# The order of all operations as a searched list in place of a list scheduler; bonus sums on quarters of the array, a combine over four row groups, the first unit in four loads

## The chip, the cores and the metric

One NeuronCore of a Trainium2 chip runs the kernel. The metric is the device time of one execution in microseconds; shorter is better. Two executions that differ by less than some 2% can't be told apart here.

## The reference

A linear-attention layer (one decaying state per head) is followed by a soft mixture of experts. All tensors are f32: batch 4, 8 heads, 768 steps, head dimension 48, so the second part sees 3072 tokens of 384 features, with 8 experts of 4 slots and hidden size 1024.

```python
for t in range(S):                          # attention, per batch and head
    cur = einsum('bhd,bhe->bhde', u[None] * kt, vt)
    y[:, :, t] = einsum('bhd,bhde->bhe', rt, state + cur)
    state = wt[:, :, :, None] * state + einsum('bhd,bhe->bhde', kt, vt)
...
logits = x @ phi                            # mixture, over all 3072 tokens
d = softmax(logits, axis=0); slot_input = d.T @ x
slot_out[e] = maximum(slot_input[e] @ w1[e], 0) @ w2[e]
out = softmax(logits, axis=1) @ slot_out
```

## The kernel before

**The attention** is cut into 6 chunks of 128 steps and worked on in 16 pairs of heads, four per batch. Decays, keys and receptances come in 12 units (three per batch; each holds one pair and a third of the batch's fourth pair, which small transfers gather later). A unit is loaded as `wu` (387 KB) and `kru` (774 KB, keys and receptances side by side); VectorE makes running products of the decays (`F` and `E`, scans at L896 and L902, a reciprocal between them) and multiplies keys and receptances by them in place (`KR`, L908). Since `KR` overwrites its input, it waits for GpSimd's product of receptances and keys (`rk`, L893), from which TensorE makes the bonus sums (`bonus`, L917; ScalarE copies them out, L921).

Each pair then does on TensorE: `sc` (scores of a half, L1012, twice), `kn` (keys turned, L966), `U` (outer products of the chunks, L985), `AV` (scores by values, L1030, twice) and `in` (the part from the state, L1042). Between them ScalarE copies scores out (`at`, L1018), GpSimd masks them (`mask`, L1020) and scales values (`av`, L994), VectorE scans the states (`S`, L989) and adds up the pair (`y`, L1046). After four pairs the batch goes through the first part of the mixture: transposes (`xT`, L320), logits (`lg`, L336), a running maximum and exponentials, and slot sums (`smm`, L383); row softmaxes on the side (`rows`, `rsub`, `rmul`).

**The tail** spreads the slots (L450 to L482), multiplies by the first expert weights (`up`, L496), turns the result, multiplies by the second (`down`, L556, in three column groups of 160, 160 and 64), copies the rows to four places (`rep`, L566) and combines (`mix`, L582: six products of 32 rows by 128 columns per call, two row groups at a time, four calls per column group, in turn in two tiles of two banks, `cu` and `yp`). Evictions (L593, L595) and twelve output transfers follow.

**The order** is made on the host when the program is built. Each operation has an engine, a cost, a key (a due time) and the buffers it touches; `Plan.schedule` always takes the operation that can start first, with a slack within which the smaller key goes first, and the program is written out in that order. On the chip each engine, SyncE's transfer issues among them, works through its own list strictly in order, and waits on semaphores. `Plan.fill` puts products of zeros (L1211) into TensorE's longer planned gaps. PSUM has four single banks (`tp`), and the tiles `cu` and `yp`. The first unit is loaded and worked on in two halves of its columns; a half of `kru` is two separate strips of the tile (keys and receptances).

## Time and profile before

| what | value |
| --- | --- |
| median of 3 runs | 234.37 us (233.75 to 237.42) |
| profiled execution, its own time | 235.6 us |
| its span, first to last instruction | 233.9 us |
| TensorE / VectorE / GpSimd / ScalarE busy | 195.7 / 113.3 / 90.4 / 77.3 us |
| mean granted TensorE clock | 0.907 of 2.4 GHz |
| moved by DMA | 52.01 MB |

TensorE's busy time holds 21.7 us of products of zeros, and products that ran at half the clock. The engines' clocks and times below all come from the one profiled execution; a place is given in microseconds from the start of its span.

### The profile page before, as it was taken

To read this page: it belongs to the slowest core of one execution; us is meant where nothing else is said; L and a number is where in the kernel's file an instruction comes from. 1 tells how busy PE (TensorE), PEld (TensorE's weight loads), DVE (VectorE), ACT (ScalarE), POOL (GpSimd) and SP (SyncE) were. 2 spreads that over 40 slices of the span, in tenths; PEclk is the share of its full clock that TensorE was granted. 3 is DMA by queue.
4 is the path that set the end of the run, shared out by engine and by line. 5 is a ranking of instruction groups with operands and counts; after the bars stand their busy time and mean duration, and the time that the engine had idled before them with its cause. 6 is when DMAs were issued, how large, how long until landed. Compare 5 with 4: busy or idle time off the path is not lost.

```text
span 233.9 us, 9696 instructions
## 1 busy us (share of the span) xinstructions
PE 195.7 (84%) x4357; PEld 147.7 (63%) x4368; DVE 113.3 (48%) x162; ACT 77.3 (33%) x215; POOL 90.4 (39%) x126
## 2 busy tenths in 40 slices
PE   7379799888999787998978998979778889999870
PEld 2177667768757677865767884858665232588760
DVE  6196449775675375189547566352111310334340
ACT  0233215451525333343534655335312200313130
POOL 1256612842518575451757781384523000000000
PEclk9965979996899995899999999999958979999995
DMA  4799967998879699381656332129942935967193
GB/s 136 267 400 340 331 251 235 347 343 250 226 241 369 156 365 358 131 224 53 188 100 219 99 87 38 53 36 314 356 197 29 372 141 159 418 236 280 63 354 134
DMA packets 16049, 52.01 MB, mean 222 GB/s; under 512 B 2304, under 2 KB 3584, under 8 KB 16000
## 3 DMA queue, kind: packets, MB, share of 16 engines
q1 hardware_dynamic: 16000, 51.31, 65.1%
q8 instruction: 36, 0.59, 1.0%
q14 instruction: 13, 0.11, 0.2%
HBM read 44.21 MB, written 4.72 MB: 209 GB/s over the span
## 4 chain that ended last, share of the span: by engine, by line
PE 68%; POOL 9%; issue 7%; DMA 5%; DVE 4%; ACT 4%; SPq 0%; DVEq 0%; POOLq 0%
PE bank L1012 13%; PE bank L1030 11%; PE bank L1042 7%; POOL arena L1020 5%; PE bank L496 5%; PE bank L556 5%; PE bank L320 4%; PE bank L985 4%; PE bank L966 4%; DMA arena<-in_kru_dram 4%; PE bank L582 3%; PE bank L917 3%; PE bank L1211 3%; PE bank L336 2%; PE bank L383 2%
## 5 line engine op out<-in xcount | busy, mean ns | idle before, releaser
L1020 POOL TENSOR_SCALAR_AFFINE_SELECT arena<-arena 128x384 f32<-128x384 f32 x64 | 42.2, 683 | 61.6 <-ACT arena L1018 61.6
L1018 ACT COPY arena<-bank 128x384 f32<-128x384 f32 x64 | 27.5, 483 | 49.6 <-PE bank L1012 49.6
L1012 PE MATMUL bank<-arena 48*64 48x128 f32 x768 | 36.5, 306 | 7.2 <-issue 6.9
L1030 PE MATMUL bank<-arena 128*64 128x48 f32 x768 | 33.2, 236 | 7.3 <-POOL arena L1020 5.0
L1030 PEld LDWEIGHTS bank<-arena 128*64 128x64 f32 x768 | 28.7, 149 | 13.8 <-POOL arena L1020 7.9
L1012 PEld LDWEIGHTS bank<-arena 48*64 48x64 f32 x768 | 27.2, 151 | 13.8 <-issue 10.0
L908 DVE TENSOR_TENSOR arena<-arena 128x1548 f32<-128x1548 f32 (+1 forms) x13 | 24.6, 1893 | 7.8 <-POOL arena L893 7.2
L1046 DVE TENSOR_TENSOR arena<-bank,arena 128x576 f32<-128x576 f32 x16 | 12.0, 753 | 32.0 <-PE bank L1042 32.0
L893 POOL TENSOR_TENSOR arena<-arena 128x774 f32<-128x774 f32 (+1 forms) x13 | 18.9, 1453 | 21.8 <-PE bank L917 12.8
L989 DVE TENSOR_TENSOR_SCAN arena<-bank,arena 112x288 f32<-112x288 f32 x16 | 12.0, 749 | 26.1 <-PE bank L985 24.2
L1211 PE MATMUL bank<-zb 128*128 128x512 bf16 x69 | 21.7, 433 | 2.7 <-DVE bank L823 1.3
L896 DVE TENSOR_TENSOR_SCAN arena<-arena,bank 128x774 f32<-128x774 f32 (+1 forms) x13 | 21.2, 1633 | 1.3 <-DMA arena<-in_wu_dram 1.3
L902 DVE TENSOR_TENSOR_SCAN arena<-arena,bank 128x774 f32<-128x774 f32 (+1 forms) x13 | 21.3, 1640 | 0.4
L994 POOL TENSOR_TENSOR arena<-arena 128x576 f32<-128x576 f32 x16 | 18.5, 1156 | 1.5 <-ACT arena L921 1.4
L1042 PE MATMUL bank<-arena 48*64 48x48 f32 x640 | 17.9, 267 | 0.7 <-issue 0.7
L1042 PEld LDWEIGHTS bank<-arena 48*64 48x64 f32 x640 | 14.6, 150 | 1.9 <-issue 1.1
L917 PE MATMUL bank<-ub,arena 128*64 128x4 f32 x288 | 11.4, 208 | 5.0 <-DMA ub<-in_ub_dram 5.0
L966 PE MATMUL bank<-ident,arena 48*64 48x48 f32 x640 | 14.4, 234 | 0.9 <-issue 0.9
L917 PEld LDWEIGHTS bank<-ub,arena 128*64 128x64 f32 x288 | 10.6, 152 | 6.6 <-POOL arena L893 5.5
L966 PEld LDWEIGHTS bank<-ident,arena 48*64 48x64 f32 x640 | 13.8, 151 | 1.3 <-issue 1.0
L324 ACT COPY arena<-bank 128x384 f32<-128x384 f32 x24 | 10.6, 491 | 11.9 <-PE bank L320 11.9
L1211 PEld LDWEIGHTS <-zb 128*128 128x128 bf16 x80 | 7.7, 107 | 10.7 <-issue 4.8
(107 smaller groups left out, 211.3 us busy)
## 6 DMA issues: line engine op xcount, KB each, us to landing
arena<-in_w_dram SPq DMA_DIRECT2D x24, 512.0 KB, 7.7
arena<-in_w_dram SPq DMA_DIRECT2D x16, 640.0 KB, 6.6
arena<-in_kru_dram SPq DMA_DIRECT2D x11, 774.0 KB, 6.5
arena<-in_vp_dram SPq DMA_DIRECT2D x16, 288.0 KB, 3.3
arena<-in_wu_dram SPq DMA_DIRECT2D x11, 387.0 KB, 5.1
out_dram<-arena SPq DMA_DIRECT2D x8, 480.0 KB, 4.2
arena<-arena SPq DMA_DIRECT2D x24, 96.8 KB, 3.4
arena<-in_w_dram SPq DMA_DIRECT2D x8, 256.0 KB, 7.6
```

Source lines behind the costliest of these rows:

```text
L893: pl.op("POOL", 1.83 * wd / UW, lambda lo=lo, hi=hi: nc.gpsimd.tensor_tensor(out=rk.t[:, lo:hi], in0=r_of()[:, lo:hi], in1=k_of()[:, lo:hi ...
L896: pl.op("DVE", 0.07 + 1.7 * wd / UW, lambda lo=lo, hi=hi: nc.vector.tensor_tensor_scan(out=F_OF(q)[:, 1 + lo:1 + hi], data0=E_OF(q)[:, lo: ...
L902: pl.op("DVE", 0.07 + 1.7 * wd / UW, lambda lo=lo, hi=hi: nc.vector.tensor_tensor_scan(out=E_OF(q)[:, lo:hi][:, ::-1], data0=E_OF(q)[:, lo ...
L908: nc.vector.tensor_tensor(out=both(kr.t, lo, hi), in0=both(kr.t, lo, hi), in1=fac, op=ALU.mult)
L917: nc.tensor.matmul(out=ap.t[64 * th:64 * th + 64, c * 4:c * 4 + 4], lhsT=chunk(rk.t, c)[:, 64 * th:64 * th + 64], rhs=ub[:, j, :], start=T ...
L966: nc.tensor.matmul(out=kps[h].t[cols, c * D:(c + 1) * D], lhsT=chunk(K_OF(head(h)), c)[:, cols], rhs=ident[head(h), head(h)], start=True, ...
L1012: nc.tensor.matmul(out=aps[h].t[cols, cc * P:(cc + 1) * P], lhsT=chunk(K_OF(head(h)), 3 * hf + cc)[:, cols], rhs=chunk(R_OF(head(h)), 3 * ...
L1018: pl.op("ACT", 0.49, lambda h=h, aps=aps, ats=ats: nc.scalar.copy(out=ats[h].t, in_=aps[h].t[:, 0:3 * P]), r=[aps[h]], w=[ats[h]], key=kk, ...
L1020: pl.op("POOL", 0.55, lambda h=h, ats=ats: nc.gpsimd.affine_select(out=ats[h].t.rearrange("p (c t) -> p c t", c=3), in_=ats[h].t.rearrange ...
L1030: nc.tensor.matmul(out=yp.t[cols, 512 * h + c * D:512 * h + (c + 1) * D], lhsT=ats[h].t[:, cc * P + 64 * th:cc * P + 64 * th + 64], rhs=v4 ...
L1042: nc.tensor.matmul(out=yp.t[cols, 512 * h + c * D:512 * h + (c + 1) * D], lhsT=chunk(R_OF(head(h)), c)[:, cols], rhs=se[head(h), :, c], st ...
L1211: nc.tensor.matmul(out=tile[:, 0:512], lhsT=zb[:, 0:P], rhs=zb, start=True, stop=True)
```

## The change

1. `Plan.schedule` and all keys, due times and slacks go. `ORDER`, a constant list of the 788 operations by number, is written into the kernel, and `arrange` only replays it: it gives out the buffers and works out the planned times, which `fill` needs for the products of zeros. Costs of many operations are restated (for example `in` 0.58 to 0.80, `mask` 0.55 to 0.60), transfers are planned at most eight deep, and `near` adds a dependence, in the planned times alone, between `y` and `xT` of one batch.
2. `bonus`: 12 products of all 128 rows become 24 of 64 rows, in four quarters of the array, into two banks rather than one, with two copies by ScalarE.
3. `mix`: the four calls per column group become two, each of 12 products over four row groups; the first goes to `cu` and `yp`, the second to all four `tp` banks.
4. The first unit's `kru` comes in four pieces, each one strip of the tile, and `KR` of that unit is done for keys and receptances apart. Decoded, the list begins SyncE's queue with `wu` of unit 0 in two halves, `wu` of unit 1, `ub`, `kru` of unit 1, values of pair 1, and then the four pieces; TensorE's begins with `bonus1`, `sc1.0`, `sc0.0`. On GpSimd the row softmax of the first batch (`rsub0`) comes after the masks of pair 11 and those of batches 1 and 2 after the last pair; on TensorE `lg2`, `dturn2`, `smm2` and `rows1` stand between the steps of batch 3 (`AV15.1`, `xT3.0.1`, `lg2`, two more `xT3`, `in15`, `xT3.0.0`, `dturn2`, two more `xT3`, `lg3`, `smm2`, `rows1`, `dturn3`, `spread`, `rows3`, `smm3`, `den`, `slots`, `up00`); in the tail the order is `down00`, `down01`, `down10`, `rep0`, `down11`, `mix0.0`, `cturn1`, `rep1`, `mix1.1`, `mix1.0`, `down20`, `down21`, `fsum`, `mix0.1`, `rep2`, `mix2.0`, `mix2.1`.

```diff
-    def schedule(self):
+    def arrange(self, order):
...
+        for n in order:
+            o = self.ops[n]
+            assert all(p in done for p in o.preds), o.name
+            t = free[o.eng]
             for h in o.allocs:
...
+            for p in near.get(o, ()):
+                if p in done:
+                    t = max(t, reach(p, o.eng))
...
+            if o.eng == "SP":
+                if len(sent) >= self.DEEP:
+                    t = max(t, sent[-self.DEEP].end)
+                sent.append(o)
...
+            if n == 0:
+                for m in range(2):
+                    pl.op("SP", 0.42, dma(lambda lo=lo, hi=hi, m=m: q["kr"].t[:, m * UW + lo:m * UW + hi],
+                                          kru[n][:, m * UW + lo:m * UW + hi]), w=[(q["kr"], (i, m))],
+                          name=f"ld_kr{n}.{i}{m}", kb=(hi - lo) * 0.65)
+                continue
...
-                    nc.tensor.matmul(out=ap.t[64 * th:64 * th + 64, c * 4:c * 4 + 4], lhsT=chunk(rk.t, c)[:, 64 * th:64 * th + 64],
-                                     rhs=ub[:, j, :], start=True, stop=True)
+                    for h in range(2):
+                        cols, rows = slice(64 * th, 64 * th + 64), slice(64 * h, 64 * h + 64)
+                        nc.tensor.matmul(out=aps[h].t[cols, 2 * c:2 * c + 2], lhsT=chunk(rk.t, c)[rows, cols],
+                                         rhs=ub[rows, j, 2 * h:2 * h + 2], start=True, stop=True)
...
+                mx = [pl.new("tp") for _ in range(4)] if i else [pl.new("cu"), pl.new("yp")]
...
+                def mix(i=i, mv=mv, lo=lo, wd=wd):
+                    for j in range(3):
+                        for q in range(4):
+                            rows_ = slice(32 * q, 32 * q + NS)
+                            nc.tensor.matmul(out=mv(q)[:, j * wd:(j + 1) * wd], lhsT=cT[rows_, (3 * i + j) * P:(3 * i + j + 1) * P],
+                                             rhs=parts[rows_, lo:lo + wd], start=(j == 0), stop=(j == 2))
```

## Rows read from the trace of the kernel before

**Rows 1.** Busy time by stretch: length, engines (instructions), clock, DMA share, GB/s

```profile
14.80:27.30 12.50, 12.17 (x305) 10.80 (x307) 8.25 (x7) 5.21 (x15) 7.81 (x9) 0.66 1.03 344
27.30:178.30 151.00, 131.21 (x3306) 105.17 (x3310) 82.47 (x93) 59.85 (x169) 77.39 (x98) 0.92 0.64 208
102.70:140.10 37.40, 33.46 (x917) 26.73 (x919) 24.20 (x29) 16.41 (x47) 22.27 (x27) 1.00 0.47 134
178.30:189.50 11.20, 8.42 (x61) 4.34 (x63) 3.64 (x12) 2.49 (x8) 1.81 (x1) 1.00 0.84 281
201.70:228.20 26.50, 23.41 (x552) 20.16 (x552) 10.87 (x30) 7.84 (x21) 0.00 (x0) 1.00 0.65 255
```

**Rows 2.** The same of L1211, the products of zeros, alone

```profile
27.30:178.30 151.00, 11.36 (x38) 4.16 (x47) 0.92 0.64 208
178.30:189.50 11.20, 2.82 (x10) 0.98 (x11) 1.00 0.84 281
```

**Rows 3.** The chain that ended last: start, length, what; its longest waits for nothing seen

```profile
27.50 2.04 issue
...
51.80 1.57 issue
...
86.80 2.20 issue
...
168.38 2.64 issue
```

**Rows 4.** Busy time by stretch of 2 us after the last of these waits

```profile
170.00:172.00 2.00, 0.98 (x13) 0.72 (x12) 0.00 (x0) 0.00 (x0) 0.00 (x0) 0.50 1.00 409
...
176.00:178.00 2.00, 2.00 (x64) 1.92 (x62) 0.00 (x0) 0.39 (x1) 0.00 (x0) 0.80 0.00 0
```

**Rows 5.** DMA queue that brings instructions, from the page: packets, MB, share

```profile
q8 instruction: 36, 0.59, 1.0%
```

**Rows 6.** Instructions in order of time at the head: start, length, engine [idle before]

```profile
3.34 0.96 DVE L896 TENSOR_TENSOR_SCAN arena<-arena,bank 128x387 f32<-128x387 f32 x1 [0.75 <-DMA arena<-in_wu_dram]
...
5.74 0.57 SPq L819 DMA_DIRECT2D arena<-in_kru_dram  x1
...
9.72 0.87 POOL L893 TENSOR_TENSOR arena<-arena 128x387 f32<-128x387 f32 x1 [8.15 <-DMA arena<-in_kru_dram]
...
10.63 0.97 DVE L908 TENSOR_TENSOR arena<-arena 128x774 f32<-128x774 f32 x1 [5.12 <-POOL arena L893]
...
14.66 1.76 DVE L896 TENSOR_TENSOR_SCAN arena<-arena,bank 128x774 f32<-128x774 f32 x1
...
14.80 1.56 PE L1012 MATMUL bank<-arena 48*64 48x128 f32 x24 [0.17 <-DVE arena L908]
```

**Rows 7.** Waits of SyncE's queue: waited for, us in total, times, longest

```profile
SPq L819 <- DMA arena<-in_kru_dram: 4.7, 2, 3.1
```

**Rows 8.** The chain around pair 9, where GpSimd holds it

```profile
113.25 1.16 POOL arena L994
114.41 1.52 POOL arena L893
...
116.40 2.49 POOL arena L1020 x2
```

**Rows 9.** Instructions in order of time in the tail: down (128, 64), mix

```profile
203.60 4.57 PE L556 MATMUL bank<-arena 128*32 128x160 f32 x128
...
209.58 1.48 PE L582 MATMUL bank<-arena 32*128 32x160 f32 x24
...
225.22 1.17 PE L582 MATMUL bank<-arena 32*128 32x64 f32 x24 [0.39 <-DVE arena L569]
```

**Rows 10.** The chain at full clock: scores, keys turned, bonus

```profile
158.28 0.66 PE bank L1012 x24
158.94 0.57 PE bank L966 x40
...
162.07 0.66 PE bank L917 x24
```

More of the change, by code (lines that the diff above doesn't have):

```diff
@@ L44 @@
 N_OWN = 8
-SLOT = 6.2
-LEAD = 0.0
-MOE = (1.0, 4.0, 6.0, 7.0)
+ORDER = tuple(int(x) for x in """
[25 rows of a table added]
+""".split())
 class Handle:
@@ L164, in places @@
-                if best is None:
-                    return None
-                got.append(best)
-            return got
-        def start_of(o):
-            t = max(free[o.eng], o.nb)
-            for h in o.touch:
-                if h not in o.allocs and h.ring.name != "fx":
-                    if h.t is None:
-                        return None
-                    t = max(t, h.since)
+                        best = (a, m)
+                a, m = best
+                held[h.ring][m] = h
@@ L232, in fill @@
             for h in self.rings[n].handles:
-                taken.setdefault((n, h.buf), []).append((min(o.start for o in h.ops), max(o.end for o in h.ops)))
-        extra, t, past = [], first, []
+                if h.ops:
+                    spans = [(o.start, o.end, at[o]) for o in h.ops]
+                    taken.setdefault((n, h.buf), []).append((min(x[0] for x in spans), max(x[1] for x in spans),
+                                                             min(x[2] for x in spans), max(x[2] for x in spans)))
+        extra, t, past = {}, first, []
         for o in [x for x in self.order if x.eng == "PE"]:
@@ L243, in fill @@
                 for place, busy in taken.items():
-                    if all(b < t - 0.1 or a >= o.start for a, b in busy):
+                    if all(b < t - 0.1 and q < at[o] or a >= o.start and p >= at[o] for a, b, p, q in busy):
                         f = Op()
                         f.start, f.name, f.eng, f.cost = o.start - 0.05 - n * self.FILL, f"fill{n}", "PE", n * self.FILL
-                        f.end, f.key = f.start + f.cost, 0
+                        f.end = f.start + f.cost
                         tile = self.rings[place[0]].tiles[place[1]]
                         f.fn = lambda n=n, tile=tile: make(n, tile)
-                        extra.append(f)
+                        extra[o] = f
                         past.append((o.start, n * 0.213))
@@ L254, in fill @@
             t = max(t, o.end)
-        self.order = sorted(self.order + extra, key=lambda o: o.start)
+        order = []
+        for o in self.order:
+            if o in extra:
+                order.append(extra[o])
+            order.append(o)
+        self.order = order
     def run(self):
@@ new lines, in moe_tail, with oev @@
+                pl.op("PE", 6 * wd * 0.00084 + 0.05, mix, r=[("cT", i), ("parts", cg)],
+                      w=mx if i else [(h, m) for h in mx for m in range(2)], mode="r32", name=f"mix{cg}.{i}")
+                o = outs[cg]
+                dst = out[:, NT * lo:NT * hi].rearrange("p (i q m) -> p i q m", i=2, q=4)
+                for q in range(4):
+                    def oev(q=q, mv=mv, o=o, i=i):
+                        to = o[:, i, q].rearrange("p j d -> p (j d)")
+                        if q % 2:
+                            nc.scalar.copy(out=to, in_=mv(q))
+                        else:
+                            nc.vector.tensor_copy(out=to, in_=mv(q))
+                    pl.op("ACT" if q % 2 else "DVE", 0.09 + 3 * wd * (0.00098 if q % 2 else 0.00116), oev,
+                          r=[mx[q] if i else (mx[q // 2], q % 2)], w=[(f"o{cg}", (i, q))], name=f"oev{cg}.{i}{q}", after=ups)
@@ L881, in run_unit @@
         b, j = divmod(n, UNITS)
-        key = unit_key(n)
-        rk, a, ap = pl.new("rk"), pl.new("a"), pl.new("tp")
+        rk, a, aps = pl.new("rk"), pl.new("a"), [pl.new("tp") for _ in range(2)]
         q["a"] = a
```

472 lines of the change are left out of this document (173 added, 299 removed), and 25 rows, old and new, of the table ORDER.

## The prediction

> **What bounds the kernel now.** I read the profile in this order: the busy times by stretch, to see where TensorE works and where not; the same for the products of zeros, since these count as busy and do nothing; the chain of work that ended last, for what holds TensorE in the rest; the granted clock; and the order of time at both ends.
>
> Between 27.3 and 178.3 us, the loop over pairs, TensorE is busy 131.21 of 151.0 us [rows 1], 11.36 of them with zeros [rows 2]: 119.85 useful and 31.15 not. In the one batch that ran at full clock throughout it is 33.46 of 37.4 [rows 1]. So TensorE is the bound of the loop, with a fifth of its time lost. The loss has two parts. In the chain, four waits for nothing that the profile shows sum to 8.45 us [rows 3]; all four lie where the DMA engines are full, and after each the clock is at half (1.2 instead of 2.4 GHz) for some microseconds: after the last one, whole 2 us stretches stand at 0.50 and it comes back between 176 and 178 [rows 4]. That is about 6 us at half, or 3 us lost; one such event costs about 2.1 + 2.8 = 4.9 us. The other 31.15 - 8.45 = 22.7 us are waits on other engines, and the place to read them is where GpSimd holds the chain: around pair 9 it does `av`, then the next unit's `rk`, a step of the row softmax, and only then two masks in 2.49 us, for which `AV` waits [rows 8].
>
> At the head, the first scores start at 14.80. The second half of the first `kru` is issued only at 5.74 [rows 6], since SyncE waits for the landing of the first half (4.7 us in two waits, the longest 3.1 [rows 7]): each half is two strips of the tile, and the spans of the two halves overlap. Then GpSimd starts at 9.72, and VectorE has stood idle for 5.12 us [rows 6]. From 14.8 to 27.3 TensorE has work nearly all the time, but at a mean clock of 0.66 [rows 1]. The chain from the last pair to `up` (178.3 to 189.5) holds 8.42 - 2.82 = 5.60 us of useful work in 11.2 [rows 1, 2], the tail 23.41 in 26.5 [rows 1].
>
> **The change part by part.** (All terms are on the profiled execution's span of 233.9 us.)
>
> Head. The pieces of `kru` no longer overlap, so the transfers are issued one behind the other, and VectorE's hole takes both scans of unit 1 (2 x 1.76, rated from [rows 6]). Unit 1's `kru` is the fifth transfer; it and what stands ahead are 1.55 MB, of which the first 0.19 MB were there at 3.34 [rows 6]; the rest at the 344 GB/s of full DMA [rows 1] takes 4.0 us: 7.3 at the earliest, and at the latest the 9.7 at which the last `kru` piece was there before. Then `rk` over two half widths (2 x 0.87) and `KR` (2 x 0.97) [rows 6] give first scores at 11.0 to 13.4, against 14.80. I take -3.0, near the early end, since the wait that made the late end is what the edit removes. TensorE's rest before its first products shrinks with it, so part of the half clock goes: 34% of 12.5 us is lost clock pulses, 4.3 us if TensorE is the bound; I take -2.0 (0 to -4.3). Queued behind the new first transfers on SyncE are the values of pair 0, which now come after two more units; `AV0.0` waits for them, and this is in the range of the head.
>
> Loop. The new list has the row softmax of the first batch's `rsub` behind the masks of pair 11 and the other batches' after the last pair, and the masks of a pair mostly ahead of `av` and of the next `rk`. The block of [rows 8] is 2.41 + 2.49 us, of which I give 2.4 back: the masks could start once `av` alone is done (or before it) rather than after `rk`. The chain has a second block of this kind one batch later. The lookahead of two pairs that the list shows on TensorE should fill part of the smaller ones. What it can take at most is 22.7, or two thirds of that if the batch at full clock is a measure (37.4 - 33.46 + 1.83 = 5.77 lost per batch even there). I take -9 for the loop: two blocks, 4.8, and a quarter of the remaining 17.9. The bounds are -3 and -15. Within the chain to `up`, 5.6 us are free, and the list puts `lg2`, `smm2` and smaller steps there, some 3.5 us that leave the loop: -3.0 (0 to -5).
>
> `mix`. Two calls of 24 products (the f32 instruction counts) took 1.48 us at width 160 and 1.17 at width 64 [rows 9], so all six pairs of calls cost about 4 x 1.48 + 2 x 1.17 = 8.3, less some overlap at their ends. The operation in four groups that the trace does show is `down` (column groups): 128 products in 4.57, or 36 ns each at width 160. At that rate a new call is 24 x 0.036 = 0.86 and the six are 4 x 0.86 + 2 x 0.35 = 4.1. The gain lies between 0 (weights of 128 columns are loaded one after another) and that 4.2; nearly all on the chain; I take -3.0, since the row nearest to it is `down`. The waits between calls for evictions go, as both calls have their own banks: -1.5 of the tail's 26.5 - 23.41 = 3.1. New there: the second call holds all four `tp` banks, and `down20`, `rep` and the flag product queue behind its evictions.
>
> `bonus`. 24 products in 0.66 us become 48. The row nearest in form is `kn`, in quarters as well: 40 in 0.57, or 14 ns each at width 48; scores in quarters are 27.5 ns at width 128 [rows 10]. Going on along that line to width 2 gives 6.6 ns, so 48 x 6.6 to 48 x 14.2 = 0.32 to 0.68, a gain of 0.34 to a loss of 0.02 per unit. I take -0.21, or -2.5 for twelve. The second bank and the second copy by ScalarE hide behind an engine that is a third busy; if they don't, the next `sc`, which needs two banks, waits 0.2 per unit: 2.4. By the Trainium skill (TensorE: Matmul & The Clock Gate, Part 1) starts never come closer than about 25 ns however narrow the product; by that 48 would take 1.2 us and the sum would be 9 higher. The 14 ns of `kn` disagree.
>
> The DMA engines. The same bytes must move in a shorter time, so I expect one more event of the kind in [rows 3, 4]: +5 (0 to +20). That the wait is for instructions is my reading: TensorE waits for no semaphore, and a queue of 36 packets brings instructions past the same engines [rows 5]. The Trainium skill (Runtime: NRT & Kernel Launch, Instruction fetch mechanics) says that such fetches are hidden behind the issue of instructions; the 2 us waits speak against it here. By that rule this term would be nil.
>
> Sum: -3.0 - 2.0 - 9.0 - 3.0 - 3.0 - 1.5 - 2.5 + 5.0 = -19.0. The span would be 214.9. The profiled execution took 1.7 more than its span (235.6), the median is 234.37, so the profile stands for the median within 0.5%; 234.4 - 19.0 = 215.4.
>
> **The rivals.** (a) The list saves no waits in the loop: the planned times know nothing of the DMA events nor of two masks that take 2.49 us beside other work, and every late step holds a whole queue. Against it: the block of [rows 8] is gone from the list by its order alone. Then -9 and -3 fall away: 227.4. (b) It takes two thirds of the loop's waits and adds no event: 215.4 - 6 - 5 = 204.4. (c) `mix` and `bonus` don't do what they say, weight loads being the bound: 215.4 + 5.5 = 220.9. (d) Narrow products in quarters start no faster than the scores' 27.5 ns: 48 take 1.32, each bonus is 0.66 dearer, and the sum is 2.5 + 7.9 higher: 225.8; the rows of `kn` speak against it. This is the skill's floor of starts as a mechanism of this kernel. (e) The waits of [rows 3] don't follow the DMA load, so none is added: 210.4. This is what the skill's page on the runtime would make of it. (f) Slower: DMA events. The list puts pieces of the first expert's weights among the loads of the first units, and fills the DMA engines up for longer; each event costs 4.9. With five events above the four of now, four above what the sum holds, all is given back (235); with six it is 240. It decides from there, and for it speaks only that four such events came with a DMA share of 0.64 over the loop.
>
> **How the numbers follow.** The forecast 50%, with its own range 208 to 221; (a) 18%, around 222 to 232 with its bounds; (b) 10%; (c) 7%; (d) 3%; (e) 5%; (f) 7%. Two per cent, about what can be told from no change, is 229.7 to 239.1. Faster: the forecast, (b) to (e) and nearly half of (a), 0.83; within: the rest of (a), 0.10; slower: 0.07. The range leaves out the upper part of (a) and (f) above and half of (b) below: 204 to 230.
>
> **What would show it.** First scores at 11 to 13 us, at a clock near 1; SyncE without the wait for `kru`; fewer zeros and less idle time on TensorE up to the last `y`, which ends near 165 instead of 179; `mix` near 0.86 us a call; bonus near 0.45. Wrong would make it: more than five waits of 2 us with half clock behind them; masks that still come late behind `rk`; first scores after 13.4.

## The result and the profile after

The changed kernel took 228.58 us, median of four runs (222.13 to 233.45), beside 234.06 for the kernel before in the same session: 0.955 of its time, with a 95% interval of 0.941 to 0.970. (Here and below a ratio with an interval leaves out disturbed runs of either kernel; the medians of all runs give 0.977, and two later sessions gave 0.975 and 0.976 by medians.) The forecast was 215.4, with a range of 204 to 230: the kernel is faster, as said, but by 5.5 us of the 19 by medians, and by 10.3 in the profiled execution. That execution took 225.31 us, with a span of 223.6 against 233.9 before.

Where the 10.3 us came from is read by landmarks, found in the order of time of either trace:

| stretch | before | after | difference |
| --- | --- | --- | --- |
| start to the first scores | 14.80 | 12.56 | -2.2 |
| first scores to the end of the last `y` | 164.3 | 156.6 | -7.7 |
| last `y` to `up` | 10.4 | 9.2 | -1.2 |
| `up` to `down` | 14.1 | 14.1 | 0 |
| `down` to the last product | 24.1 | 22.2 | -1.9 |
| last product to the end of the span | 6.2 | 8.9 | +2.7 |

The second stretch is the one to look into. First the kernel before: busy times by stretch (length, then the time and count of TensorE, its weight loads, VectorE, ScalarE and GpSimd, then granted clock, DMA share and GB/s); the second line holds the products of zeros alone.

```profile
14.80:179.10 164.30, 143.38 (x3607) 115.96 (x3617) 91.48 (x100) 65.06 (x183) 85.97 (x107) 0.90 0.67 217
...
14.80:179.10 164.30, 12.00 (x39) 4.29 (x49) 0.90 0.67 217
```

The same view of the kernel after, with the zeros of the loop as its second line, then the chain to `up`:

```profile
12.56:169.18 156.62, 142.49 (x3820) 124.35 (x3820) 88.82 (x92) 65.35 (x187) 80.65 (x103) 0.76 0.69 223
...
12.56:169.18 156.62, 1.92 (x4) 0.39 (x4) 0.76 0.69 223
...
169.18:178.40 9.22, 7.97 (x69) 4.46 (x71) 3.61 (x14) 3.22 (x12) 0.00 (x0) 1.00 0.78 261
```

Take the zeros from the busy time and the busy time from the length. Before: 131.4 us of useful products, 12.0 of zeros, 20.9 idle. After: 140.6 useful, 1.9 zeros, 14.1 idle. So idle and zeros, which answer to [rows 1, 2], fell by 16.9 us, and the useful products grew by 9.2, though some 2 us of them had moved behind the last `y` and the others are the same but for the form of the bonus. The column of the clock has the reason: 0.90 against 0.76. The split is that of one execution; in two later profiles of the same kernel idle and zeros were 21.9 and 16.0 us, the useful products 134.8 and 148.6.

What TensorE still waits for, in the list of its waits (waited for, us in total, times, longest):

```profile
PE bank L1005 <- issue: 6.2, 4, 2.7
...
PE bank L1034 <- issue: 2.1, 3, 1.0
PE bank L1022 <- issue: 1.9, 2, 1.3
PE bank L1005 <- ACT arena L1010: 1.6, 1, 1.6
...
PE bank L313 <- ACT arena L317: 0.8, 1, 0.8
```

In the loop only the 1.6 us are a wait on another engine; the 0.8 stand behind the last `y`. "issue" is time in which it waits for nothing that the profile shows, the kind of [rows 3]. All waits on GpSimd are gone from the loop; at the place that answers to [rows 8] the masks now stand ahead of `av`, in order of time:

```profile
95.27 0.99 POOL L1012 TENSOR_SCALAR_AFFINE_SELECT arena<-arena 128x384 f32<-128x384 f32 x2 [2.83 <-ACT arena L1010]
96.23 1.16 POOL L987 TENSOR_TENSOR arena<-arena 128x576 f32<-128x576 f32 x1
```

And the clock, as stretches of 2 us. It fell at 11.9 and came back at 46.0, though TensorE counts as busy nearly all of that time (27.78 of the 28 us from 18 to 46); this answers to [rows 4], where half clock lasted some 7 us.

```profile
16.00:18.00 2.00, 2.00 (x61) 2.00 (x59) 1.88 (x4) 0.66 (x2) 0.14 (x2) 0.50 1.00 372
...
28.00:30.00 2.00, 2.00 (x57) 1.99 (x56) 0.93 (x2) 0.46 (x2) 1.45 (x2) 0.50 0.95 200
34.00:36.00 2.00, 2.00 (x37) 1.41 (x31) 1.60 (x3) 0.00 (x0) 0.89 (x1) 0.50 0.42 86
...
46.00:48.00 2.00, 2.00 (x96) 1.95 (x96) 0.92 (x2) 1.46 (x5) 1.19 (x3) 0.99 0.23 54
```

From the first scores to the last product the granted clock was at half for 79.2 us after, against 35.7 before (lengths of the clock's own records added up). Of the 79.2 us, 33.5 lie in the head; 10.2 begin at 59.7, in a stop of 2.7 us; 6.8 and 23.9 begin at 90.4 and 107.5, behind stops of only 0.49 and 0.67; the other 4.8 lie behind the last `y`.

**Where the stops lie.** If the instructions of TensorE (products, weight loads and those of its sequencer) are counted in order of time, every stop of 0.6 us or more in the loop of the changed kernel that has no engine's name behind it comes at number 191 of a block of 256, and the queue that brings instructions moves one packet of 16,384 bytes for each such block (38 packets in all, against 36 in [rows 5]). In the kernel before it is 183 to 192, falling with time as records are missing from its trace (of the loop's zeros it has 49 weight loads but 39 products). So these are waits for the next block of instructions; those of 0.5 us or more sum to 10.6 us up to the last `y`, and to 10.6 in the kernel before. They did not grow. In the trace of after, TensorE entered a block at 54.0; the packet of the next one ran from 57.83 to 58.70; TensorE stopped at 57.5 and went on at 60.21, 1.5 us after the packet. It is the same everywhere: at each of the 105 such stops of 0.5 us or more in the fourteen traces of this case (from 4 us behind the first scores to the last `y`), TensorE went on 1.2 to 1.7 us after the end of a packet of this queue. In order of time, the starts behind this stop and the one before it:

```profile
54.02 0.32 PE L1005 MATMUL bank<-arena 48*64 48x128 f32 x1 [1.80 <-issue]
...
60.21 1.34 PE L1005 MATMUL bank<-arena 48*64 48x128 f32 x19 [2.74 <-issue]
```

The Trainium skill (Runtime: NRT & Kernel Launch, Instruction fetch mechanics) gives the same block, 16 KiB or 256 instructions, fetched over a DMA queue of the engine's own; that crossing a boundary is "mostly hidden" does not hold here, where nine stops cost the 10.6 us.

### The profile page after: what moved, and what is told of

Its sections match the earlier page's. It is cut to its first block, busy times and chain, and to the rows that moved or that the text cites. A ratio compares the mean times of both kernels' runs of the same rounds, so it can differ in the third digit from the quotient of the medians.

```text
span 223.6 us, 10211 instructions
## 1 busy us (share of the span) xinstructions
PE 192.4 (86%) x4602; PEld 154.4 (69%) x4605; DVE 114.5 (51%) x164; ACT 79.1 (35%) x227; POOL 88.8 (40%) x126
## 5 line engine op out<-in xcount | busy, mean ns | idle before, releaser
L1012 POOL TENSOR_SCALAR_AFFINE_SELECT arena<-arena 128x384 f32<-128x384 f32 x64 | 37.9, 611 | 41.8 <-ACT arena L1010 41.6
L1010 ACT COPY arena<-bank 128x384 f32<-128x384 f32 x64 | 29.6, 483 | 48.5 <-PE bank L1005 31.3
L1005 PE MATMUL bank<-arena 48*64 48x128 f32 x768 | 39.6, 345 | 7.8 <-issue 6.2
L1005 PEld LDWEIGHTS bank<-arena 48*64 48x64 f32 x768 | 30.5, 175 | 11.8 <-issue 7.6
L1022 PEld LDWEIGHTS bank<-arena 128*64 128x64 f32 x768 | 32.9, 176 | 5.4 <-issue 4.9
L873 POOL TENSOR_TENSOR arena<-arena 128x774 f32<-128x774 f32 (+1 forms) x13 | 20.5, 1580 | 29.9 <-issue 14.1
L1038 DVE TENSOR_TENSOR arena<-bank,arena 128x576 f32<-128x576 f32 x16 | 12.1, 757 | 33.0 <-PE bank L1034 27.9
L898 DVE TENSOR_TENSOR arena<-arena 128x1548 f32<-128x1548 f32 x11 | 21.9, 1994 | 10.4 <-POOL arena L873 10.2
L1034 PEld LDWEIGHTS bank<-arena 48*64 48x64 f32 x640 | 16.9, 167 | 3.7 <-issue 3.4
L909 PEld LDWEIGHTS bank<-ub,arena 64*64 64x64 f32 x576 | 13.0, 164 | 6.0 <-POOL arena L873 3.8
L909 PE MATMUL bank<-ub,arena 64*64 64x2 f32 x576 | 13.6, 212 | 3.7 <-POOL arena L873 3.3
L960 PE MATMUL bank<-ident,arena 48*64 48x48 f32 x640 | 16.1, 251 | 0.8 <-issue 0.8
L982 DVE TENSOR_TENSOR_SCAN arena<-bank,arena 112x288 f32<-112x288 f32 x16 | 11.9, 747 | 9.1 <-PE bank L978 6.5
L965 ACT COPY arena<-bank 128x240 f32<-128x240 f32 x32 | 10.1, 365 | 16.4 <-PE bank L960 16.3
L978 PE MATMUL bank<-arena 128*48 128x48 f32 x320 | 12.7, 237 | 0.0
```

Source lines behind the costliest of these rows:

```text
L873: pl.op("POOL", 1.83 * wd / UW, lambda lo=lo, hi=hi: nc.gpsimd.tensor_tensor(out=rk.t[:, lo:hi], in0=r_of()[:, lo:hi], in1=k_of()[:, lo:hi ...
L898: nc.vector.tensor_tensor(out=both(kr.t, lo, hi), in0=both(kr.t, lo, hi), in1=fac, op=ALU.mult)
L909: nc.tensor.matmul(out=aps[h].t[cols, 2 * c:2 * c + 2], lhsT=chunk(rk.t, c)[rows, cols], rhs=ub[rows, j, 2 * h:2 * h + 2], start=True, sto ...
L960: nc.tensor.matmul(out=kps[h].t[cols, c * D:(c + 1) * D], lhsT=chunk(K_OF(head(h)), c)[:, cols], rhs=ident[head(h), head(h)], start=True, ...
L1005: nc.tensor.matmul(out=aps[h].t[cols, cc * P:(cc + 1) * P], lhsT=chunk(K_OF(head(h)), 3 * hf + cc)[:, cols], rhs=chunk(R_OF(head(h)), 3 * ...
L1010: pl.op("ACT", 0.49, lambda h=h, aps=aps, ats=ats: nc.scalar.copy(out=ats[h].t, in_=aps[h].t[:, 0:3 * P]), r=[aps[h]], w=[ats[h]], name=f" ...
```

## The experiments

Theory: the new list took nearly all waits on other engines; part of what it gained was lost again to half clock (time at 1.2 of 2.4 GHz), which begins behind late instruction blocks (those for which TensorE stops) and at the cold head (the first products, which started at half clock), and lasts since the loop's products are narrow and few zeros are left. Rivals: the parts (`mix`, bonus, head) and not the list made the gain; a block costs the same whatever the DMA engines do; half clock has nothing to do with the stops.

**Zeros in the head, and in the whole loop.** The filler, which puts zeros where the planned times leave a gap, is given a least number at some places.

```
+FORCE = {'bonus1': 32, 'sc1.0': 6, 'sc0.0': 8, 'kn1': 4, 'bonus0': 5, 'AV0.0': 4, 'kn0': 3, 'sc0.1': 2}
...
+            n = max(n, FORCE.get(o.name, 0))
             if n > 0:
```

> The changed kernel with more products of zeros ahead of its first eight operations on TensorE (32 ahead of the first bonus sum, 6, 8, 4, 5, 4, 3 and 2 ahead of the next ones), nothing else. Theory A, the clock: TensorE rests between 7.2 and 10.5 us, falls to half clock at 12 and stays there until 46 although it is busy all the time; work that could run at twice the speed sets the pace. With the rest filled the clock should stay at full until the first longer wait near 52, and some 10 to 15 us of the 34 at half come back: 210 to 215 us. Theory B, the others: VectorE, the transfers and the order hold the first 46 us anyway; the clock rises but the time stays within 2 us of the changed kernel's 222 to 225.

Measured: 227.93 us (224.39 to 229.87) beside 238.60 for the kernel before on that chip, 0.955 by medians, 0.981 [0.968, 0.994]. The 210 to 215 us of theory A did not come. By stretch, first scores onward, and then the two places in order of time behind which the clock fell:

```profile
13.09:25.59 12.50, 12.21 (x265) 7.25 (x266) 11.38 (x11) 4.56 (x14) 7.05 (x8) 1.00 0.83 281
...
31.68 1.02 PE L1013 MATMUL bank<-arena 48*64 48x128 f32 x24 [2.65 <-issue]
...
46.12 0.99 PE L968 MATMUL bank<-ident,arena 48*64 48x48 f32 x27 [2.44 <-issue]
```

The head is mended, 1.00 instead of 0.50 in its first 12.5 us (changed kernel: 10.65 us busy with 227 products there), and the third `y` was out at 44.3 instead of 48.6. Then two late blocks came, half clock behind them from 32.3 to 35.7 and from 46.0 to 73.3, and by the eighth `y` the lead had turned into a lag of 2.9 us. In this trace a head kept warm gave its gain back at the next late blocks.

The same with four more zeros ahead of each bonus from the fourth unit on:

> As warm_head, and in addition four products of zeros ahead of each bonus sum of units 3 to 11 (36 more, 0.21 us each at full clock, 7.7 us in sum). Theory A: the long stretches at half (12 to 46, 60 to 70, 107 to 131) go or end early; mean clock over 0.92 and 205 to 212 us, since the zeros cost less than the half clock. Theory B: TensorE is the bound and the clock is not, or the list has no room: 2 to 8 us slower than warm_head. If the falls come from waits for instructions alone, the clock still falls near 60, 90 and 107 but comes back sooner.

Measured: 233.33 us over ten runs (228.37 to 236.51), 0.978 by medians, 0.986 [0.974, 0.998]; it is 5.4 over the warm head alone, as theory B had it. Half clock was 51.2 us in the profiled run instead of 61.4, but the 36 zeros and the stops (seven of 1.2 us or more up to `up`) took more than that gave. Zeros put down blindly don't pay.

**The parts without the list.** The three parts (`mix` over four row groups, bonus in quarters, first unit in four transfers), as in the change, on the kernel before with its own scheduler; for example

```
-                    nc.tensor.matmul(out=ap.t[64 * th:64 * th + 64, c * 4:c * 4 + 4], ...
+                    for h in range(2):
+                        cols, rows = slice(64 * th, 64 * th + 64), slice(64 * h, 64 * h + 64)
+                        nc.tensor.matmul(out=aps[h].t[cols, 2 * c:2 * c + 2], lhsT=chunk(rk.t, c)[rows, cols],
+                                         rhs=ub[rows, j, 2 * h:2 * h + 2], start=True, stop=True)
```

> The kernel before with the three parts (four loads of the first unit, bonus sums in quarters, combine over four row groups), under its old list scheduler and keys. By the sum of the prediction the parts are worth 3 (head), 3 + 1.5 (combine) and up to 2.5 (bonus): 224 to 229 us. Rival: the order is all that counts and the parts are hidden: 232 to 235. Rival: the parts are all of the gain and the list adds nothing: 221 to 225.

Measured: 233.60 us over ten runs (229.37 to 236.95) beside 238.60 on that chip, 0.979 by medians; first scores at 13.07, the tail from `down` to the last product 22.2 us. So the parts alone give, by medians, about what the whole change gives (0.975 to 0.977), though on other chips, and the 5.0 us are just under the 5.4 to 10.4 that 224 to 229 us mean beside 234.4. What the parts are worth without the list is not settled by this: on the same chip the list with the parts and the warm head took 227.93, and the lowest of the ten runs here, 229.37, lies above the lowest 227.22 of the kernel before. TensorE's costliest groups, by form (line, tile, partitions x elements, count, then busy us and mean ns, then idle time before them), `mix` and bonus with the parts:

```profile
L937 PE MATMUL bank<-ub,arena 64*64 64x2 f32 x576 | 11.8, 203 | 6.2 <-DMA ub<-in_ub_dram 4.7 <-issue 1.5
...
L581 PE MATMUL bank<-arena 32*128 32x160 f32 x96 | 3.8, 302 | 0.4 <-DVE arena L568 0.4
...
L581 PE MATMUL bank<-arena 32*128 32x64 f32 x48 | 1.6, 274 | 0.3 <-DVE arena L568 0.3
```

and the same groups of the kernel before:

```profile
L917 PE MATMUL bank<-ub,arena 128*64 128x4 f32 x288 | 11.4, 208 | 5.0 <-DMA ub<-in_ub_dram 5.0
...
L582 PE MATMUL bank<-arena 32*128 32x160 f32 x96 | 6.2, 310 | 0.8 <-DVE arena L595 0.8
...
L582 PE MATMUL bank<-arena 32*128 32x64 f32 x48 | 2.3, 278 | 0.5 <-DVE arena L569 0.4 <-DVE arena L595 0.2
```

`mix` fell from 8.5 to 5.4 us; the bonus went from 11.4 to 11.8, so it gained nothing. From `down` to the last product, at full clock in both, TensorE was idle for 3.7 us with the parts and for 2.6 before.

**Less for the DMA engines to do, and loads in step.** Four kernels on one chip. The first is the changed kernel itself.

> The changed kernel once more, as the measure for the three beside it. Both theories: the same time as at its first timing, 222 to 233 us, and again about ten stops of TensorE of 0.6 us or more in the loop, about 13 us in all, each where TensorE passes into a new block of 256 instructions, with some 70 to 80 us at half clock.

Measured: 229.82 us (224.27 to 230.99) beside 235.66. In the profiled run the stops at block ends summed to 16.1 us and half clock to 64.3, where 70 to 80 were expected.

```
-                pl.op("SP", 0.4, dma(lambda ...: h.t[:, lo:hi], w1[n][:, lo:hi]), ...
+                pl.op("SP", 0.4, dma(lambda ...: h.t[:, lo:hi], w1[n][:, lo:hi]) if n == E - 1 else lambda: None, ...
...
-                                rhs=wts[e].t[:, kt * F + hf * 512:...
+                                rhs=wts[E - 1].t[:, kt * F + hf * 512:...
```

> Leaves out part of the transfers: of the first layer's weights only the last expert's are loaded, and its weights stand in for all eight, so 11 of some 41 MB that move before the products of the first layer are gone and nothing on TensorE changes. Theory (the stops are late instruction blocks, held up behind data in the DMA engines): at most four stops of 0.6 us or more in the loop instead of ten, under 5 us in all, and half clock down from 78 us to 35 to 50 (the first stretch from 12 us on stays, it began with narrow products and not with a stop); 207 to 217 us. Rival 1 (a new block costs the same whatever the DMA engines do): ten stops, within 2% of the changed kernel. Rival 2 (the half clock comes from the narrow products alone and the stops only go with it): stops fall to under 5 us but half clock stays above 65 us; 217 to 222.

Measured: 218.40 us (213.26 to 222.45), 11.4 under the changed kernel beside it, and half clock down to 43.7 us: most of what the theory said. But the stops didn't go as it said: up to the last `y` five instead of eight, 12.4 us instead of 16.1. Fewer loads did not empty the DMA engines where it counted: at the four stops of 2.2 to 3.5 us their share was 0.91 to 0.99 from the entry into the block before to the start of the packet, and at the fifth, of 0.7 us, 0.15.

```
+        def go():
+            if len(sent) >= 1:
+                nc.sync.dma_start(out=pace[0:1, len(sent):len(sent) + 1], in_=sent[-1])
+            nc.sync.dma_start(out=dst(), in_=src)
+            sent.append(dst()[0:1, 0:1])
```

> The same bytes, but each piece of the first layer's weights is sent only when the piece before it has landed (a transfer of one number that reads the earlier piece stands ahead of it in SyncE's queue; 23 such waits). Theory: less data stands ahead of an instruction block, so the stops fall to under 8 us in all and half clock with them; 213 to 222 us. Rival (SyncE's waits hold up the loads of the units and values queued behind them): masks and scores wait for loads, the first products of the first layer start after 178 us, and the time is 229 or more.

Measured: 234.44 us (232.55 to 238.91), against 229.82. The stops fell to 7.2 us, as the theory had it, and the rival took it back. TensorE's waits:

```profile
PE bank L989 <- DMA arena<-in_vp_dram: 8.4, 2, 5.3
PE bank L1016 <- issue: 6.2, 4, 2.9
```

SyncE stood 59.7 us behind the weights, the values of two pairs behind SyncE, and TensorE 8.4 us behind the values; half clock came to 89.7 us. The last `y` came 8 us later than in the changed kernel.

> The paced loads, and 64 products of zeros at eight places of the head that keep TensorE busy until the second pair (with these alone the clock was full up to 32 us, and then fell behind two stops of 2.65 and 2.44 us). Theory: the two need each other; with fewer stops the clock of the head is kept, half clock is under 40 us in all, and the time is 203 to 214 us, at least 5 under the paced loads alone. Rival (zeros only shift the half clock to a later place): within 2% of the paced loads alone.

Measured: 230.52 us (230.38 to 231.19): 3.9 under the paced loads alone, no better than the changed kernel, and half clock 81.9 us instead of the expected under 40. The expectation fell; the rival's 2% holds.

**One place, and all at once.** Again four kernels on one chip, the first the changed kernel.

> The changed kernel once more, as the measure for the three beside it: 222 to 233 us on any chip seen so far, with stops of TensorE at block ends of 13 to 18 us in the loop and 75 to 80 us at half clock.

Measured: 232.50 us (226.01 to 234.52) beside 238.15. In its profiled run (span 232.8) the stops summed to 12.1 us and half clock to 101.6.

```
-                pl.op("SP", 0.45, dma(...), w=[(h, cg)], name=f"ld_x{i}.{cg}", ...
+                pl.op("SP", 0.45, (lambda: None) if i < 3 else dma(...), w=[(h, cg)], name=f"ld_x{i}.{cg}", ...
...
-                                rhs=wts[E + e].t[:, ...
+                                rhs=wts[E + max(e, 3)].t[:, ...
```

> Leaves out the loads of the second layer's weights of the first three experts (nine transfers, 4.7 MB, that move from about 145 us on; the fourth expert's weights stand in for them). A local test: in both runs with these loads TensorE stopped for 3.3 us at the block end that lies at 149 us in the changed kernel (136 in the one with fewer loads of the first layer), with the instruction block fetched 4.2 us after TensorE had crossed the boundary before. Theory (blocks wait behind data): that stop goes and the next boundary's too, with the half clock behind them (156 to 163), while the stops before 140 us stay in number and size; 4 to 7 us in all. Rival (the place in the program, or a fixed cost of a block): the stop at that boundary stays at 2 us or more, and the time is the same within 1%.

Measured: 229.20 us (224.63 to 230.37), 3.3 under the changed kernel beside it, with ranges that overlap. The time says little; the place says more. Half clock behind it, from 156 to 163 in the first of the two repeats of the changed kernel and from 164 to 171 in the second, is gone: the clock is full from 136.6 to 181.0. And the stop is shorter, always ahead of the last nine products of the same `AV`. In order of time, the first repeat of the changed kernel:

```profile
155.37 0.49 PE L1022 MATMUL bank<-arena 128*64 128x48 f32 x9 [3.27 <-issue]
```

The second repeat:

```profile
164.14 0.77 PE L1022 MATMUL bank<-arena 128*64 128x48 f32 x9 [2.99 <-issue]
```

Without the second layer's loads that move there:

```profile
160.02 0.49 PE L1022 MATMUL bank<-arena 128*64 128x48 f32 x9 [1.35 <-issue]
```

Beside them the packet of the block, from the records of the instruction queue, for all executions that bear on it (the last line is the kernel of the next paragraph), with the DMA share from the time TensorE entered the block before to the packet's start:

```
run                            enters block  packet from  to       DMA share   enters next  stop
changed kernel, first profile  152.18        154.32       155.55   1.02        156.93       1.29
changed kernel, 1st again      148.80        153.02       154.00   0.94        155.37       3.27
changed kernel, 2nd again      157.84        161.78       162.80   0.95        164.13       2.99
fewer first-layer loads        136.29        140.52       141.53   0.95        142.87       3.33
no second-layer loads there    155.37        157.82       158.78   0.46        160.02       1.35
neither, and a warm head       136.60        137.73       138.89   0.15        140.28       1.00
```

The shares are from the busy times by stretch. The changed kernel, 1st again:

```profile
148.80:153.02 4.22, 3.30 (x126) 3.12 (x125) 1.90 (x3) 2.32 (x6) 2.99 (x6) 1.00 0.94 329
```

and without the second layer's loads:

```profile
155.37:157.82 2.45, 2.45 (x106) 2.39 (x105) 1.55 (x3) 0.41 (x2) 1.93 (x4) 1.00 0.46 186
```

The packet takes 1.0 to 1.2 us and TensorE goes on 1.2 to 1.4 us after it, in every run; what differs is when the packet starts: 2.1 to 4.2 us after TensorE has entered the block before while the DMA engines are full, 2.5 and 1.1 when they have room. So a load in the way can make a block late by up to 3 us and need not. The 105 stops of all traces say the same: at each of the 45 of 1.7 us or more the DMA share, taken in this way, was 0.84 or more, and of the eight with a share under 0.7 none was longer than 1.35 us. And 1.1 + 1.2 + 1.4 = 3.7 us remain, while at full clock TensorE was through those 256 instructions in 2.7: a stop of 1.0 us stays when no load stands in the way. The rival had a part of the truth.

> Leaves out the loads of all but one expert's first-layer weights and those of the first three experts' second layer, and has the 64 products of zeros in the head that keep the clock full up to the second pair: what the new order does when the DMA engines have room and the head is warm. Theory (stops and half clock have eaten the gain): stops under 8 us in the loop, half clock under 40 us, last y before 152 us, 198 to 208 us in all. Rival (the half clock is the lot of the new order, whose products are narrow and which has few zeros): half clock stays over 55 us and the time over 212.

Measured: 209.04 us (205.49 to 219.89), 23.5 under the changed kernel beside it. By stretch, first scores to last `y`, with the zeros in the second line:

```profile
13.40:152.90 139.50, 124.53 (x3841) 105.11 (x3843) 87.36 (x92) 65.18 (x187) 77.55 (x102) 0.95 0.50 144
...
13.40:152.90 139.50, 6.79 (x25) 2.15 (x27) 0.95 0.50 144
```

The useful products took 117.7 us, against 140.6 in the changed kernel and 131.4 in the kernel before; idle were 15.0 us, against 14.1. Stops at block ends: eleven, 12.2 us, hardly less than the 10.6 to 16.1 of the changed kernel and not the "under 8" expected, but all except one of 3.0 were under 1.4. Half clock: 13.7 us, where the rival had over 55; the last `y`, at 152.9, and the time just miss the theory's 152 and 208. So the DMA engines and the head cost the new order some 17 us between first scores and last `y`, and they cost them through the clock, not as idle time; how much of it is the head's, no run separates. The clock in 40 slices of the span (tenths), from the page of the kernel before,

```profile
PEclk9965979996899995899999999999958979999995
```

from that of the changed kernel,

```profile
PEclk9955555589857999589655579999999969999955
```

and from that of this one:

```profile
PEclk9999999999959999999769999999999999999995
```

**The bonus in its old form.** 24 products of full height, width 4, in place of 48 quarters of width 2; the order as in the change.

```
-                    for h in range(2):
...
-                        nc.tensor.matmul(out=aps[h].t[cols, 2 * c:2 * c + 2], lhsT=chunk(rk.t, c)[rows, cols],
-                                         rhs=ub[rows, j, 2 * h:2 * h + 2], start=True, stop=True)
+                    nc.tensor.matmul(out=aps[0].t[cols, 4 * c:4 * c + 4], lhsT=chunk(rk.t, c)[:, cols],
+                                     rhs=ub[:, j, :], start=True, stop=True)
```

> The changed kernel with the bonus in its old form, 24 products of full height and width 4 in place of 48 quarters of width 2; the order and all else as they are. In the traces so far 24 old ones and 48 new ones take the same time from first to last start (0.63 to 0.67 and 0.63 to 0.68 us at full clock, 1.20 and 1.16 to 1.29 at half), so the products themselves should change nothing. Theory (instruction blocks): 576 fewer instructions on TensorE are two and a quarter blocks fewer, so one or two stops fewer, and time lower by 2 to 6 us. Rival (the quarters were worth the predicted 2.5 us, or nothing): the time is the same within 1% or up to 3 us higher.

Measured: 224.63 us (220.43 to 228.96), 7.9 under the changed kernel beside it and more than the 2 to 6 expected, but with stops of 17.6 us instead of 12.1, so not through fewer stops. In one unit another product wrote the bank between the two copies, so that the second copy waited for it and took its sums; it ran once more with one copy:

```
-            pl.op("ACT", 0.19, lambda h=h: nc.scalar.copy(out=a.t..., in_=aps[0].t...[:, :, 2 * h:2 * h + 2]), ...
+            pl.op("ACT", 0.19, lambda h=h: None if h else nc.scalar.copy(out=a.t, in_=aps[0].t[:, 0:4 * C]), ...
```

> The changed kernel with the bonus as 24 products of full height and one copy out of one bank (in the run before this one, the copies of one unit read a bank that had been given on, so that run's output was off; here one copy reads all 24 columns). It has 576 instructions fewer on TensorE and the order of the change. Theory (fewer instruction blocks, so fewer late ones, and less time at half clock): 0.93 to 0.955 of the kernel before, against 0.955, 0.975 and 0.976 for the changed kernel at its three timings, with 50 to 75 us at half clock, and this would be the fastest complete version. Rival (the bonus in quarters is worth nothing and costs nothing): 0.96 to 0.98. Second rival (the quarters gain the predicted 2.5 us): 0.97 or more.

Measured: 226.59 us over six runs (222.83 to 230.31) beside 234.50: 0.966 by medians, where the changed kernel had 0.975 to 0.977. That is in the first rival's range. The stops weren't fewer either (18.1 us). Half clock was 51.2 us, inside the expected 50 to 75. Whether this version is faster than the changed kernel by the 1% between them isn't settled: by the lowest runs it has 0.970 of the kernel before, the changed kernel 0.953, 0.976 and 0.963.

**All traces together.** Half clock between the first scores and the last product, how much of it lies up to the last `y`, the useful products and the stops without an engine's name (0.5 us or more) up to the last `y`, and the time of the last product:

```
run                       half clock  to last y  useful  stops  last product
before                          35.7       32.3   131.4   10.6         227.7
parts, old list                 38.7       38.7   131.9    7.3         221.0
changed kernel                  79.2       74.4   140.6   10.6         214.7
changed kernel, 1st again       64.3       61.4   134.8   16.1         213.7
changed kernel, 2nd again      101.6       95.7   148.6   12.1         224.4
warm head                       61.4       61.4   135.5   12.9         213.8
fewer first-layer loads         43.7       37.5   125.7   12.4         202.5
no second-layer loads           81.5       75.3   141.0   12.5         217.9
neither, warm head              13.7       13.7   117.7   12.2         196.0
paced loads                     89.7       85.4   143.9    7.2         223.0
paced loads, warm head          81.9       78.5   142.0    3.7         220.5
zeros in head and loop          51.2       51.2   128.4   16.6         221.9
old bonus, two copies           54.1       50.7   130.7   17.6         211.4
old bonus, one copy             51.2       47.8   130.4   18.1         211.8
```

In the twelve traces with the new list the useful products lie on a line, 111.4 us and 0.39 for each us of half clock, within 1.1 us but for the run with zeros in the whole loop (2.7 under it). So in these traces half clock tells what the products take. The sum of the stops tells nothing of the time of the last product; half clock goes with it, but for that same run, whose 18.7 us of zeros in the loop kept it down. Of the 105 stops of all fourteen traces, the 45 of 1.7 us or more all began at full clock, and at 40 of them the clock fell during the stop or up to 2 us behind it; of the 38 between 0.5 and 1.2 us that began at full clock only 8 had this. What full DMA engines can do is to turn a stop of the second kind into one of the first. It is not all: in the changed kernel's own first profile only 10.2 of the 79.2 us at half begin at a stop of the first kind.

## Why the prediction was right in its range and wrong in its sum

- **Head, -3.0.** Right: -2.2, first scores at 12.56 within 11.0 to 13.4. SyncE issued four pieces of `kru` one behind the other without a wait ([rows 7] has no successor), and GpSimd started at 8.88 instead of 9.72 [rows 6]:

```profile
3.62 2.10 SPq L798 DMA_DIRECT2D arena<-in_kru_dram  x4
...
8.88 1.55 POOL L873 TENSOR_TENSOR arena<-arena 128x774 f32<-128x774 f32 x1 [6.64 <-DMA arena<-in_kru_dram]
...
10.49 0.88 PE L909 MATMUL bank<-ub,arena 64*64 64x2 f32 x48 [3.30 <-POOL arena L873]
```

- **Clock at the head, -2.0.** This step failed. It reasoned that a shorter rest before the first products would keep the clock; TensorE still rested 3.3 us, then had products of width 2, and the clock stayed at half for 34 us where [rows 1] had a mean of 0.66. The named sign, first scores at a clock near 1, came out as 0.50.
- **Loop waits, -9 (-3 to -15).** Right in kind, mis-sized: of the 22.7 us of zeros and waits on other engines (20.6 if every stop of the kind of [rows 3] is taken out) some 2.3 are left: the loop from 25.1 to 169.2 is 144.1 us long, 131.8 of them busy and 0.6 of these with zeros, and 10.6 are stops. So 18 to 20 came, beyond the bound of 15. That bound was two thirds of the 22.7, but the figure beside it, 5.77 us lost in a batch at full clock, is 23.1 for four batches and does not lead there. Nor does [rows 8] give the 2.41 us of the prediction: `rk` and the step behind it take 1.99, from 114.41 to 116.40. Rival (a) has nearly the right time, 227.4, for a reason that is wrong.
- **One more event, +5 (0 to +20).** This step failed: the term was too small, and built on the wrong quantity. It priced a stop with 2.8 us lost to half clock behind it and counted stops. Stops at block ends are 10.6 us in both kernels, so not even that event came, nor the sign of more than five stops of 2 us: there was one. The half clock is what grew, from 35.7 to 79.2 us, in stretches of up to 34 us where the kernel before had at most 10. In the loop its price is 11.2 us: the useful products grew by 9.2 though 2.0 had moved out. With room for the DMA engines and a warm head the same products took 117.7, 22.8 less. The Trainium skill (TensorE: Matmul & The Clock Gate, HAM oscillation) puts the penalty at half of the throttled time; by that, as an estimate, 43.5 us more would have cost 21.8. The traces give less, 0.39 for each us over the twelve with the new list. By that line the 42.1 us more up to the last `y` would be 16 and not 11; the old order's useful products lie 7.6 us above the line (131.4, where it gives 123.9), 2.0 of which are the work that moved, and what the others are was not traced.
- **Chain to `up`, -3.0.** About right: it holds 7.97 - 0.38 (zeros) = 7.6 us of useful work where 5.6 stood [rows 1, 2], so 2.0 have left the loop for it, and it is 1.2 shorter itself.
- **`mix`, -3.0, and its evictions, -1.5.** `mix` is right where it ran at full clock: -3.1 with the parts alone. The evictions failed there: the idle time of that tail grew by 1.1 us, with waits of 0.78 on ScalarE's copies behind two of the three column groups, so that 1.9 of the 4.5 came. In the changed kernel two calls of the last third ran into half clock (212.5 on) and one into a late block of 0.87 us, so it got 1.3 of it, 8.5 to 7.2, its idle time fell by 0.4, and the tail as a whole got -1.9. At the end SyncE issued its last output 3.5 us after the last product instead of 1.1, and the end of the span lies 2.7 us further behind that product; no step had this.
- **Bonus, -2.5.** Failed: nil. Of the two ends, 0.32 and 0.68, the line through the widths gave the first, and the row of `kn` itself, 14 ns a product [rows 10], the second. From first to last start 48 quarters took 0.63 to 0.68 us at full clock, 14 ns each, and 24 full products had taken 0.63 to 0.67. The 14 ns are the very rate of `kn`, and far from the 27.5 ns of rival (d).

By landmarks the forecast missed 8.7 of its 19.0 us: 0.8 at the head, 3.8 between first scores and last `y`, 2.6 in the tail and 2.7 behind the last product, less 1.2 that the chain to `up` gave beyond it. Between first scores and last `y` the sum had -9 for waits, -3 for work that leaves, and +0.5 for clock, bonus and event together, -11.5 in all. There came -16.9 of idle time and zeros, -2.0 of work that left and +11.2 of slower products, -7.7 in all: two errors of some 8 and 11 us that met. So that the time lies inside the range, 1.4 us under its upper end, is in part luck. The time by which the order was to make the kernel faster was there, and some two thirds of it came back as slower products.

That a stop ends behind the packet of its block is shown at all 105 stops, that long stops come where the DMA engines are full by their shares, that half clock mostly follows long stops by the count over all traces, and that useful products take longer by half clock by the line through twelve traces. That taking loads away brings time back rests on the 11.4 us that fewer loads gave and on the place that six runs share. Why half clock lasts 7 us at one time and 34 at another, with TensorE busy in both, isn't settled, and with it the larger part of the changed kernel's half clock: in the head, with the same products, it lasted 33.5, 23.9 and 24.0 us behind the first scores in the three profiles of the changed kernel and 6.8 with fewer first-layer loads. That fewer zeros prolong it is argued from the traces alone, and zeros in the whole loop shortened it by only 10 us.

## What to carry to other kernels

When an order takes the waits out of an engine that is the bound, price the work that is left at the clock it will have, and not at the one it had: here 17 us of waits and zeros went and 11 us came back as slower products. Look at where stops without a name fall, counted in instructions; if they fall at one number of 256, then a kernel of many tiny products is near the rate at which its instructions can come, and loads that fill the DMA engines can make the stops longer. Between two bounds of an unknown, take the one that a row of the same form has, not the one that a line through several forms leads to.

## What was not expected of the hardware

- At full clock TensorE ran through 256 of these instructions in 2.7 us, but the next block could start only 3.7 us after the one before had, even with a DMA share of 0.15 ahead of its packet. With a share of 0.50 over the loop, ten stops of 0.6 to 1.3 us and one of 3.0 were left in some thirty blocks.
- With full DMA engines the packet of a block started up to 4.2 us after the block before had been entered, and the stop was 3 us.
- The clock stayed at half for 34 us, in the last 28 of which the profile counted TensorE as busy for 27.78; products of zeros ahead of and between the same products kept it full up to 32.3 us.
- The same kernel, with 64, 79 and 102 us at half clock in three executions, ended its last product at 213.7, 214.7 and 224.4.
